# Two half-filled score units become one: the last 64 queries of two neighbouring head pairs share a unit

## The chip, the cores and the metric

The kernel runs on one core of one Trainium2 chip. The metric is the device time of one execution in microseconds (us). Three timed executions of the kernel before took 1442.98, 1452.02 and 1453.08 us, a median of 1452.02 us. A core has a matrix engine (TensorE, PE in the profile, with its weight loads shown apart as PEld), a vector engine (VectorE, DVE), an activation engine (ScalarE, ACT), GpSimd (POOL), and SyncE (SP), whose queue issues nearly all DMAs here. The engines run their own instruction streams and wait for each other through semaphores.

## The reference

Two stages follow each other. The first is attention with a threshold, for 8 batches of 8 heads, 576 rows of 64 numbers each:

```python
scores = scale * np.matmul(q, k.transpose(0, 1, 3, 2))
thresh = np.max(scores, axis=-1, keepdims=True) - tau
scores = np.where(scores >= thresh, scores, -1000000000.0)
attn = np.exp(scores - np.max(scores, axis=-1, keepdims=True))
attn = attn / (np.sum(attn, axis=-1, keepdims=True) + 1e-09)
return np.matmul(attn, v)
```

Its output, with the heads put side by side, is a matrix x of 4608 rows by 512. The second stage is a bilinear layer with weights w_a and w_b (512 by 1536) and w_out (1536 by 512): `((x @ w_a) * (x @ w_b)) @ w_out`. All of it is in fp32. In the records of this kernel each fp32 matmul appears as two weight loads and two matmuls, so counts in the profile are twice those in the code.

## The kernel before, in words

**Units.** The 64 heads are handled as 32 pairs, with `HP = 4` pairs to a batch. One head of a pair lies on partitions 0 to 63 (j = 0), the other on 64 to 127 (j = 1). The 576 queries of a pair are cut into four units of 128 queries and one tail unit (`u == NT`) of the last 64. The list `units` orders them, 160 in all, and the main loop `for g in range(len(units) + PV_LAG)` gives one slot to each. In the first batch the order is units 0 and 1 of all four pairs, then units 2 and 3 of each, then the four tails. In each later batch it is units 0 and 1 of the four pairs, then units 2, 3 and the tail of each.

**A unit on its engines.** `scores` (L374) issues the score matmuls on PE into PSUM, and the row maxima (L393) and thresholds (L394) on DVE. The array works as four tiles of 64 by 64: the row half is given by the head's partitions, the column half by the partitions written. A full unit has eight matmuls of 288 columns (two halves of the keys c, two groups of 64 queries t, two heads j), one to each tile and half of the keys, and fills two pairs of PSUM banks. A tail unit has only four: head 0 writes partitions 64 to 127 and head 1 writes 0 to 63, so two of the four tiles have no score matmul, and it fills one pair of banks. `weigh` then takes the exponential on ACT (L414) and applies the threshold and sums on DVE (L417); `reciprocal` and `normalise` (L436) follow. From the ninth unit on, the weights are turned by 32x32 transposes on DVE (L480), a DMA to a scratch tensor in DRAM (`turn_blocks`, swap<-tw) and a DMA back (`turn_back`, wT<-swap). Three slots after the scores (`PV_LAG`), `weighted` multiplies by v (`product`, L520) and `settle` copies the result into x tiles. What is weighted in which slot is told by `part`: half 0 of a pair after unit 1, half 1 after unit 3 in the first batch and, together with the tail, after the tail unit in later ones.

**The layer beside it.** The bilinear layer is worked off in 18 blocks of 256 rows of x (`ffn`, `sevens_of`: lines L680, L753, L810, L856). A block becomes available when its x tile is complete: two from each batch, and one more from the tails of four batches. Inside every slot `advance` issues a share of the current block's matmuls between the attention's. The share is `pace`, in moving columns: `PACE` times the columns of a block, held down so that the backlog lasts until the next block arrives (`arrivals`), plus a term for the product's columns and one for a large backlog. In the first slots the weights of the layer are also converted on ACT, POOL and DVE (`early`), some pieces per slot, through slot 15.

**Order and queues.** `keep_order` fixes every engine's instructions in the order in which the Python program issues them. DMAs are collected by `post` and released by `pump` as PE's columns go by, after slot 40; before that they are issued at once. `flush` issues what a step needs immediately. Queries of later batches arrive in two parts, q0 and q1, with `Q_BUFS = 2` buffers, three slots before they are used.

Of the kernel before, what the change touches and what calls it, by code (L numbers as in the profile page):

```python
# [10 lines left out]
FP32 = mybir.dt.float32  # L11
# [12 lines left out]
BY_PE = 8  # L24
XT_BUFS = 7
Q_BUFS = 2
OSB_BUFS = 4
PACE = 0.09
CATCH_UP = 0.05
PACE_EARLY = 0.04  # L30
ROOM = 1024
# [23 lines left out]
def kernel(  # L55
# [288 lines left out]

    prepared, scored, weights, turned, whole = {}, {}, {}, {}, {}
    x_of, xtail_of = {}, {}
    ahead, settled = {}, {}
    blocks, complete, swaps = [], [], {}

    def prep(i, name):  # L350
# [23 lines left out]
    def scores(i, u):  # L374
        qT, kT = prepared[i]["q" if i < HP else "q1" if u > 1 else "q0"], prepared[i]["k"]
        base = HALF if i >= HP and u > 1 else 0
        n = 2 if u < NT else 1
        sc = [banks(SH, "sc") for _ in range(n)]
        each = [(c, t, j) for c in range(2) for t in range(n) for j in range(2)]
        if units.index((i, u)) < BY_HEAD:  # L380
            each.sort(key=lambda x: x[2])
        for c, t, j in each:
            r = slice(j * D, (j + 1) * D)
            o = t if u < NT else 1 - j
            q0, to = (u * P + t * D if u < NT else MAIN) - base, slice(o * D, (o + 1) * D)
            nc.tensor.matmul(sc[j if u < NT else 0][to, c], qT[r, q0:q0 + D],  # L386
                             kT[r, c * SH:(c + 1) * SH], start=True, stop=True)
        mx = small.tile([P, 2], FP32, tag="mx", name="mx")
        thr = small.tile([P, 2], FP32, tag="thr", name="thr")
        bias = small.tile([P, 2], FP32, tag="bias", name="bias")  # L390
        for j in range(n):
            c = slice(j, j + 1)
            nc.vector.tensor_reduce(mx[:, c], sc[j], axis=AX.XY, op=ALU.max)  # L393
        nc.vector.tensor_scalar(thr[:, 0:n], mx[:, 0:n], cut, None, op0=ALU.subtract)  # L394
        scored[i, u] = (sc, thr, bias, mx)

    def rooms_of(i, u):


        t = work.tile([P, 2 * NB, Q], FP32, tag="tw", bufs=TW_BUFS, name="tw")  # L400
        whole[i, u] = t
        return [t[:, j * NB:(j + 1) * NB] for j in range(1 if u == NT else 2)]

    def weigh(i, u):

# [57 lines left out]
            nc.scalar.copy(wT[:, y * NT:(y + 1) * NT], tp[:, y])  # L463
        nc.vector.tensor_copy(wT[:, 2 * NT], last[:, 0])

    def part(i, u):

        if i < HP:
            return {1: (i, 0), 3: (i, 1), NT: (i, 2)}.get(u)
        return {1: (i, 0), NT: (i, 1)}.get(u)  # L470

    def width(i, h):
        return (HALF, HALF, TAIL)[h] if i < HP else (HALF, HALF + TAIL)[h]
# [1 line left out]
    def turn_blocks(i, u):  # L475

        ws, _ = weights.pop((i, u))
        t = whole.pop((i, u))
        for w in ws:
            nc.vector.transpose(w, w)  # L480
        if u < NT:
            swap = scratch.tile([G, P, NSLOT * Q], FP32, tag="swap", name="swap")
        else:
            swap = scratch.tile([2, P, NSLOT * Q], FP32, tag="swapt", name="swap")
        swaps[i, u] = swap
        for g in range(G):
            if u < NT:
                to, n = swap[g], G
            else:
                to, n = swap[g % 2, (1 - g // 2) * D:(2 - g // 2) * D], 2  # L490
            post(("tw", i, u), (to.rearrange("(r p) e -> p r e", p=Q),
                                t[g * Q:(g + 1) * Q, 0:n * NSLOT].rearrange("p (r s) e -> p r (s e)", r=n)))

    def turn_back(i, u):

        flush(("tw", i, u))
        swap = swaps.pop((i, u)).rearrange("g p e -> p g e")
        key = "wT", i, min(u // 2, 1) if i >= HP else u // 2
        if u < NT or i < HP:
            turned[i, u] = turned_tile()  # L500
            n = G if u < NT else 2
            for y in range(0, n, 2):
                post(key, (turned[i, u][:, y:y + 2].rearrange("p g s e -> p g (s e)"), swap[:, y:y + 2]))
        else:
            for y in range(2):
                post(key, (turned[i, 2 + y][:, G].rearrange("p s e -> p (s e)"), swap[:, y]))

    def join(out, lo, hi):
        nc.scalar.copy(out, lo)
# [58 lines left out]
    def weighted_unit(i, u):  # L568

        b, hp = pairs[i]  # L570
        wT = turned.pop((i, u, "pe"))
        pv = product([lambda rows, s, t=t: t[rows, s] for t in wT], loaded[i]["v"], P)
        if (b, 0) not in x_of:
            x_of[b, 0] = x_tile("xT")
            state["xs"] = x_tile("xS")
        settle(x_of[b, 0][:, hp, u * P:(u + 1) * P], pv, 0, D, ([], []))
        exchange(x_of[b, 0], state["xs"], hp, u * P, (u + 1) * P, nc.gpsimd)
        if hp == HP - 1:
            state["rows"] = u + 1
            if u == 0:  # L580
                blocks.append(((x_of[b, 0], state["xs"]), ("first", b, 0)))

    def weighted(i, h):

        b, hp = pairs[i]
        flush(("v", i), ("wT", i, h))
        n = width(i, h)
        if h < 2:
            groups = G + (n > HALF)
            wT = [turned.pop((i, 2 * h + y))[:, 0:groups] for y in range(2)]  # L590
        else:
            t = turned.pop((i, NT))
            wT = [t[:, y:y + 1] for y in range(2)]
        pv = product([lambda rows, s, t=t: t[rows, :, s] for t in wT], loaded[i]["v"], n)
        read = [], []
        if h < 2:
            if hp == 0:
                x_of[b, h] = x_tile("xT")
            settle(x_of[b, h][:, hp, :], pv, 0, P, read)
            settled[b, h] = hp + 1  # L600
            if hp == HP - 1:
                del settled[b, h]
                complete.append((x_of.pop((b, h)), ("half", b, h)))
        if n % HALF:
            t = b % GT
            if hp == 0 and t == 0:
                xtail_of[b // GT] = x_tile("xt")
            settle(xtail_of[b // GT][:, hp, t * TAIL:(t + 1) * TAIL], pv, (n - TAIL) // 2, n // 2, read)
            del loaded[i], prepared[i]
            if hp == HP - 1 and t == GT - 1:  # L610
                complete.append((xtail_of.pop(b // GT), ("tail", b - t, 0)))

# [331 lines left out]
    for i in range(0, NPR, HP):  # L944
        if i == 0:
            units += [(p, u) for u in (0, 1) for p in range(HP)]
            units += [(p, u) for p in range(HP) for u in (2, 3)]
            units += [(p, NT) for p in range(HP)]
        else:
            units += [(p, u) for p in range(i, i + HP) for u in (0, 1)]  # L950
            units += [(p, u) for p in range(i, i + HP) for u in (2, 3, NT)]
    arrivals = [g + PV_LAG + 1 for g, (i, u) in enumerate(units)
                if i % HP == HP - 1 and part(i, u) and (i >= HP or u == NT - 1)]
    first = {i: g for g, (i, u) in enumerate(units) if u == 0}
    second = {i: g for g, (i, u) in enumerate(units) if u == 2}

# [23 lines left out]
        n += size  # L980
    for g in range(len(units) + PV_LAG):
        written = len(pending)
        state["slot"], state["paced"] = g, g > 40
        while bulk and bulk[0][1] < g - 1:
            pump()
        state["converted"] = state["added"]
# [2 lines left out]
        back = ()  # L989
        if BY_PE + 1 < g <= len(units) + 1:  # L990
            n = g - PV_LAG
            back = (1 if BY_PE <= n and part(*units[n]) else 0,)
            if not back[0]:
                turn_back(*units[g - 2])
        if here:
# [4 lines left out]
        pace = (PACE if g > BY_PE else PACE_EARLY) * BLOCK_COLS  # L1000
        if g > BY_PE:
            pace = min(pace, backlog() / (min([a for a in arrivals if a > g] + [len(units) + PV_LAG + 1]) - g))
        pace += NSLOT * S / 2 / (NT + 1) + CATCH_UP * max(backlog() - BLOCK_COLS, 0)
        if 2 <= g < BY_PE + 2:
            weighted_unit(*units[g - 2])
            running["owed"] -= NSLOT * P // 2
# [13 lines left out]
            advance(PORTIONS[0] * pace)  # L1020
        for p in range(HP, NPR):
            for name, d in (("q0", 1), ("q1", 1)):
                if g == (second if name == "q1" else first)[p] - d:
                    prep(p, name)
        if here:
            weigh(i, u)
# [10 lines left out]
        if g > BY_PE:  # L1037
            n = g - PV_LAG
            held = 0.0
            if BY_PE <= n < len(units) and part(*units[n]):  # L1040
                held = 384 - (PORTIONS[2] + PORTIONS[3]) * pace + NSLOT * width(*part(*units[n])) // 2
                held = min(max(held, 0.0), 384)
            advance(PORTIONS[1] * pace - held)
            if BY_PE <= n < len(units) and part(*units[n]):
                p, h = part(*units[n])
                if pairs[p][1] == 0:
                    make_x(2 if h == 1 and p >= HP and pairs[p][0] % GT == 0 else 1)
                make_room()
                weighted(*part(*units[n]))
                passed(NSLOT * width(*part(*units[n])) // 2)  # L1050
                running["owed"] -= NSLOT * width(*part(*units[n])) // 2
            if back and back[0] > 0:
                turn_back(*units[g - 2])
        for n in early.get(g, [])[:1]:
# [14 lines left out]
        load_weights(RAWS)  # L1069
        for p in range(HP, NPR):  # L1070
            for name, d in (("q0", 3), ("k", 4), ("q1", 3)):
                if g == (second if name == "q1" else first)[p] - d:
                    load(p, name)
        for p in range(1, NPR):
            if g == first[p] - 1:
# [63 lines left out]
```

## Time and profile before

| | before |
|---|---|
| timed executions | 1442.98, 1452.02, 1453.08 us |
| profiled execution, first to last instruction | 1439.3 us |
| PE busy | 1386.8 us (96%) |
| PE weight loads busy | 1282.4 us (89%) |
| DVE busy | 1015.6 us (71%) |
| ACT busy | 683.9 us (48%) |
| POOL busy | 480.4 us (33%) |
| score matmul records L386 | 2304, 229.1 us |
| mean granted PE clock | 0.992 |

The total of the profiled execution beyond its span is not listed apart; the shortest timed execution is 3.7 us longer than the span, the median 12.7 us. Busy times of PE are modelled, since matmuls are pipelined: a matmul record of 288 columns is shown with about 405 ns, but up to four run side by side, one per tile. So a group's cost on PE has to be read from the distance between starts, not from its mean duration.

### The profile page before, as it was taken

The page shows a single profiled execution, that of the slowest core. Times are in us where ns is not written, and L with a number is a line of the kernel's source. Part 1 is how long each engine was busy: PE and PEld are TensorE (multiplying, and loading weights), DVE is VectorE, ACT ScalarE, POOL GpSimd, SP SyncE. Part 2 cuts the span into 40 slices and gives each one's busy share as a digit, 9 for nine tenths or more (in the row PEclk, how much of TensorE's full clock was granted, in tenths as well). Part 3 has the DMA queues.
Part 4 walks back from the last instruction along what each step waited for, and adds up shares of the span by engine and source line. Part 5 has one row for each costly group of instructions (what it writes and reads, how often), then busy time and mean ns, then how long its engine had stood idle before and what let it go on. Part 6 is the DMA issues. An engine that isn't in the chain of part 4 may idle for free.

```text
span 1439.3 us, 77100 instructions
## 1 busy us (share of the span) xinstructions
PE 1386.8 (96%) x34208; PEld 1282.4 (89%) x34208; DVE 1015.6 (71%) x2244; ACT 683.9 (48%) x1244; POOL 480.4 (33%) x668
## 2 busy tenths in 40 slices
PE   6888999999999999999999999999999999999998
PEld 5777798988879889989999999898898989999998
DVE  6997778788767877676757786778867776755223
ACT  5876455545545454544444545344535454430110
POOL 2763713415060605132333333240506060605000
PEclk9899999999999999999999999999999999999999
DMA  9975667667755776567545677466755686450000
GB/s 210 252 227 141 173 173 191 182 171 192 202 137 153 176 201 159 152 160 189 147 125 137 159 186 203 118 171 149 207 135 142 164 217 167 121 160 18 3 18 17
DMA packets 327004, 223.25 MB, mean 155 GB/s; under 512 B 171536, under 2 KB 310800, under 8 KB 326672
## 3 DMA queue, kind: packets, MB, share of 16 engines
q1 hardware_dynamic: 324160, 217.74, 58.5%
q8 instruction: 269, 4.41, 1.3%
q10 hardware_dynamic: 2512, 0.59, 0.2%
q14 instruction: 63, 0.52, 0.1%
HBM read 128.58 MB, written 89.65 MB: 152 GB/s over the span
## 4 chain that ended last, share of the span: by engine, by line
PE 88%; DVE 4%; DMA 4%; issue 2%; SPq 2%; ACT 1%; DVEq 0%; ACTq 0%
PE pab L680 27%; PE po L810 20%; PE pab L753 19%; PE sc L386 10%; PE pv L520 10%; PE po L856 1%; DMA wT<-swap 1%; PE tp L461 1%; DVE mx L393 1%; DVE tw L480 1%; SPq L197 1%; DMA raw<-in_moe_w_a_dram 1%; SPq L143 1%; DMA raw<-in_moe_w_b_dram 0%; DVE tw L417 0%
## 5 line engine op out<-in xcount | busy, mean ns | idle before, releaser
L436 ACT ACTIVATE tw<-tw,rcp 128x576 f32<-128x576 f32 x272 | 197.8, 769 | 228.7 <-DVE rcp L430 228.6
L393 DVE TENSOR_REDUCE mx<-sc 128x1 f32<-128x576 f32 x288 | 206.1, 752 | 140.7 <-PE sc L386 115.6
L414 ACT ACTIVATE tw<-sc,bias,scalars 128x576 f32<-128x576 f32 x288 | 239.4, 831 | 9.8 <-ACT bias L413 0.2
L646 POOL TENSOR_TENSOR h<-h,u 128x512 f32<-128x512 f32 x28 | 35.1, 1276 | 604.2 <-DVE h L723 465.4
L810 PE MATMUL po<-wo_sb,h 64*64 64x256 f32 x3264 | 230.8, 377 | 0.0
L417 DVE SCALAR_TENSOR_TENSOR tw<-sc,thr,tw 128x576 f32<-128x576 f32 x288 | 222.6, 797 | 9.7 <-ACT tw L414 9.1
L386 PE MATMUL sc<-kT,qT 64*64 64x288 f32 x2016 | 198.1, 405 | 7.2 <-issue 2.9
L480 DVE STREAM_TRANSPOSE tw<-tw 128x576 f32<-128x576 f32 x272 | 196.0, 754 | 0.8 <-ACT tw L436 0.8
L810 PEld LDWEIGHTS po<-wo_sb,h 64*64 64x64 f32 x3264 | 178.7, 133 | 15.8 <-DVE h L723 0.3
L520 PE MATMUL pv<-wT,vm 64*64 64x160 f32 (+3 forms) x5184 | 181.7, 273 | 7.1 <-issue 4.3
L520 PEld LDWEIGHTS pv<-wT,vm 64*64 64x64 f32 x5184 | 167.7, 134 | 13.9 <-issue 6.8
L810 PE MATMUL po<-sums_u,h 64*64 64x256 f32 x2448 | 169.6, 377 | 0.3 <-DVE h L761 0.3
L779 POOL TENSOR_TENSOR h<-h 128x256 f32<-128x256 f32 x168 | 117.4, 733 | 119.8 <-PE po L810 116.1
L386 PEld LDWEIGHTS sc<-kT,qT 64*64 64x64 f32 x2016 | 119.5, 133 | 31.9 <-issue 10.6
L810 PEld LDWEIGHTS po<-sums_u,h 64*64 64x64 f32 x2448 | 132.2, 133 | 12.5 <-DVE h L761 1.2
L680 PE MATMUL pab<-xU,wb_sb 64*64 64x128 f32 x4096 | 138.5, 270 | 0.1
L680 PEld LDWEIGHTS pab<-xU,wb_sb 64*64 64x64 f32 x4096 | 131.0, 133 | 2.2 <-issue 0.5
L413 ACT ACTIVATE bias<-mx,scalars 128x1 f32<-128x1 f32 x288 | 83.3, 289 | 92.5 <-DVE mx L393 92.3
L680 PE MATMUL pab<-xS,wa_sb 64*64 64x128 f32 x2048 | 113.1, 270 | 1.2 <-issue 1.2
L753 PE MATMUL pab<-xS,wb_sb 64*64 64x256 f32 (+1 forms) x1536 | 102.9, 359 | 4.1 <-issue 4.1
L527 ACT COPY xT<-pv 128x128 f32<-128x128 f32 (+1 forms) x68 | 17.6, 259 | 187.2 <-PE pv L520 152.6
L753 PE MATMUL pab<-xS,wa_sb 64*64 64x256 f32 (+1 forms) x1536 | 101.4, 361 | 0.0
(138 smaller groups left out, 2427.7 us busy)
## 6 DMA issues: line engine op xcount, KB each, us to landing
wT<-swap SPq DMA_DIRECT2D x244, 288.0 KB, 3.8
swap<-tw SPq DMA_DIRECT2D x480, 144.0 KB, 2.9
vm<-in_v_dram SPq DMA_DIRECT2D x128, 72.0 KB, 2.8
swap<-tw SPq DMA_DIRECT2D x128, 72.0 KB, 3.1
kT<-in_k_dram SPq DMA_DIRECT2D x112, 72.0 KB, 3.1
wT<-swap SPq DMA_DIRECT2D x56, 144.0 KB, 2.6
out_dram<-kept SPq DMA_DIRECT2D x30, 256.0 KB, 3.5
qT<-in_q_dram SPq DMA_DIRECT2D x112, 40.0 KB, 2.6
```

The source lines that it names most:

```text
L386: nc.tensor.matmul(sc[j if u < NT else 0][to, c], qT[r, q0:q0 + D], kT[r, c * SH:(c + 1) * SH], start=True, stop=True)
L393: nc.vector.tensor_reduce(mx[:, c], sc[j], axis=AX.XY, op=ALU.max)
L413: nc.scalar.activation(bias[:, j:j + 1], mx[:, j:j + 1], AF.Copy, scale=e_nscale)
L414: nc.scalar.activation(wb[j], sb[j], AF.Exp, bias=bias[:, j:j + 1], scale=e_scale)
L417: nc.vector.scalar_tensor_tensor(out=wv, in0=sb[j], scalar=thr[:, j:j + 1], in1=wv, op0=ALU.is_ge, op1=ALU.mult, accum_out=sums[:, j:j + 1])
L436: nc.scalar.activation(w, w, AF.Copy, scale=rcp[:, j:j + 1])
L480: nc.vector.transpose(w, w)
L520: nc.tensor.matmul(pv[c * D:(c + 1) * D, y], vm[rows, s], wT[y](rows, s), start=(s == 0), stop=(s == NSLOT - 1))
L680: nc.tensor.matmul(out[c * D:(c + 1) * D, r, f * P:(f + 1) * P], w[g][k][rows, w0:w0 + D], moving[k][rows], start=(fresh and k == 0 and f ...
L753: nc.tensor.matmul(pab[c * D:(c + 1) * D, r], w[rows, f // n, k, fs + c * D:fs + (c + 1) * D], moving, start=(k == 0), stop=(k == H - 1))
L779: (nc.vector if state["over"] else nc.gpsimd).tensor_tensor(*a, **kw)
L810: nc.tensor.matmul(po[c * D:(c + 1) * D, r, y], ht[rows, t0:t0 + D], other[rows, f], start=(f == 0), stop=(f == NF // 2 - 1))
```

## The change

The tail units of pairs p and p + 1 (p even) become one unit. It has eight matmuls of 288 columns: pair p + t writes the PSUM banks `sc[t]`, and head j of it the partitions `(j ^ t) * 64` on, so that all four tiles have score matmuls. All steps after that handle two banks as in a full unit. The joint unit stands in the list after unit 3 of the even pair: 2, 3, tail, then 2, 3 of the odd pair, in the first batch too, where the four tails stood at the end. There are 144 units instead of 160. In later batches the odd pair's half 1 and tail are now weighted after its unit 3, and its tail's scratch is read back in that unit's `turn_back`; in the first batch both pairs' tails are weighted three slots after the joint unit. The second part of an odd pair's queries is loaded and transposed one slot earlier. `PACE` becomes 0.1, the term for the product's columns follows the number of units, and the paced DMAs begin after slot 36.

```diff
-PACE = 0.09
+PACE = 0.1
 def scores(i, u):
-        n = 2 if u < NT else 1
-        sc = [banks(SH, "sc") for _ in range(n)]
-        each = [(c, t, j) for c in range(2) for t in range(n) for j in range(2)]
+        sc = [banks(SH, "sc") for _ in range(2)]
+        each = [(c, t, j) for c in range(2) for t in range(2) for j in range(2)]
...
-            o = t if u < NT else 1 - j
-            q0, to = (u * P + t * D if u < NT else MAIN) - base, slice(o * D, (o + 1) * D)
-            nc.tensor.matmul(sc[j if u < NT else 0][to, c], qT[r, q0:q0 + D],
+            if u < NT:
+                m, o, q0 = j, t, u * P + t * D - base
+            else:
+                m, o, q0 = t, j ^ t, MAIN - base
+                qT, kT = prepared[i + t]["q" if i < HP else "q1"], prepared[i + t]["k"]
+            nc.tensor.matmul(sc[m][o * D:(o + 1) * D, c], qT[r, q0:q0 + D],
                              kT[r, c * SH:(c + 1) * SH], start=True, stop=True)
...
-    def part(i, u):
+    def parts(i, u):
         if i < HP:
-            return {1: (i, 0), 3: (i, 1), NT: (i, 2)}.get(u)
-        return {1: (i, 0), NT: (i, 1)}.get(u)
+            return {1: [(i, 0)], 3: [(i, 1)], NT: [(i, 2), (i + 1, 2)]}.get(u, [])
+        return {1: [(i, 0)], NT if i % 2 == 0 else 3: [(i, 1)]}.get(u, [])
...
 def turn_back(i, u):
+        if i >= HP and u == (3 if i % 2 else NT):
+            flush(("tw", i - i % 2, NT))
+            swap = swaps[i - i % 2, NT].rearrange("g p e -> p g e")
             for y in range(2):
-                post(key, (turned[i, 2 + y][:, G].rearrange("p s e -> p (s e)"), swap[:, y]))
+                post(key, (turned[i, 2 + y][:, G].rearrange("p s e -> p (s e)"), swap[:, i % 2 * 2 + y]))
...
         if i == 0:
             units += [(p, u) for u in (0, 1) for p in range(HP)]
-            units += [(p, u) for p in range(HP) for u in (2, 3)]
-            units += [(p, NT) for p in range(HP)]
+            units += [(p, u) for p in range(HP) for u in ((2, 3) if p % 2 else (2, 3, NT))]
         else:
             units += [(p, u) for p in range(i, i + HP) for u in (0, 1)]
-            units += [(p, u) for p in range(i, i + HP) for u in (2, 3, NT)]
+            units += [(p, u) for p in range(i, i + HP) for u in ((2, 3) if p % 2 else (2, 3, NT))]
...
-        state["slot"], state["paced"] = g, g > 40
+        state["slot"], state["paced"] = g, g > 36
...
-        pace += NSLOT * S / 2 / (NT + 1) + CATCH_UP * max(backlog() - BLOCK_COLS, 0)
+        pace += NSLOT * S / (2 * NT + 1) + CATCH_UP * max(backlog() - BLOCK_COLS, 0)
...
-                if g == (second if name == "q1" else first)[p] - d:
+                if g == (second if name == "q1" else first)[p] - d - (name == "q1" and p % 2):
```

More of the change, by code (lines that the diff above doesn't have):

```diff
@@ L346 @@
     x_of, xtail_of = {}, {}
-    ahead, settled = {}, {}
+    ahead, settled, settled_of = {}, {}, {}
     blocks, complete, swaps = [], [], {}
@@ L390, in scores @@
         bias = small.tile([P, 2], FP32, tag="bias", name="bias")
-        for j in range(n):
+        for j in range(2):
             c = slice(j, j + 1)
             nc.vector.tensor_reduce(mx[:, c], sc[j], axis=AX.XY, op=ALU.max)
-        nc.vector.tensor_scalar(thr[:, 0:n], mx[:, 0:n], cut, None, op0=ALU.subtract)
+        nc.vector.tensor_scalar(thr, mx, cut, None, op0=ALU.subtract)
         scored[i, u] = (sc, thr, bias, mx)
@@ L401, in rooms_of @@
         whole[i, u] = t
-        return [t[:, j * NB:(j + 1) * NB] for j in range(1 if u == NT else 2)]
+        return [t[:, j * NB:(j + 1) * NB] for j in range(2)]
     def weigh(i, u):
@@ L480, in turn_blocks @@
             nc.vector.transpose(w, w)
[L481 to L484, printed above, removed]
+        swap = scratch.tile([G, P, NSLOT * Q], FP32, tag="swap" if u < NT else "swapt", name="swap")
         swaps[i, u] = swap
@@ L487, in turn_blocks @@
             if u < NT:
-                to, n = swap[g], G
-            else:
-                to, n = swap[g % 2, (1 - g // 2) * D:(2 - g // 2) * D], 2
-            post(("tw", i, u), (to.rearrange("(r p) e -> p r e", p=Q),
-                                t[g * Q:(g + 1) * Q, 0:n * NSLOT].rearrange("p (r s) e -> p r (s e)", r=n)))
+                moves = [(swap[g].rearrange("(r p) e -> p r e", p=Q),
+                          t[g * Q:(g + 1) * Q].rearrange("p (r s) e -> p r (s e)", r=G))]
+            else:
+                moves = []
+                for m in range(2):
+                    j = g // 2 ^ m
+                    moves.append((swap[2 * m + g % 2, j * D:(j + 1) * D].rearrange("(r p) e -> p r e", p=Q),
+                                  t[g * Q:(g + 1) * Q, m * NB:(m + 1) * NB].rearrange("p (r s) e -> p r (s e)", r=2)))
+            post(("tw", i, u), *moves)
     def turn_back(i, u):
-        flush(("tw", i, u))
-        swap = swaps.pop((i, u)).rearrange("g p e -> p g e")
         key = "wT", i, min(u // 2, 1) if i >= HP else u // 2
         if u < NT or i < HP:
+            flush(("tw", i, u))
+            swap = swaps.pop((i, u)).rearrange("g p e -> p g e")
             turned[i, u] = turned_tile()
-            n = G if u < NT else 2
-            for y in range(0, n, 2):
+            for y in range(0, G, 2):
                 post(key, (turned[i, u][:, y:y + 2].rearrange("p g s e -> p g (s e)"), swap[:, y:y + 2]))
-        else:
+        if i >= HP and u == (3 if i % 2 else NT):
+            flush(("tw", i - i % 2, NT))
+            swap = swaps[i - i % 2, NT].rearrange("g p e -> p g e")
             for y in range(2):
-                post(key, (turned[i, 2 + y][:, G].rearrange("p s e -> p (s e)"), swap[:, y]))
+                post(key, (turned[i, 2 + y][:, G].rearrange("p s e -> p (s e)"), swap[:, i % 2 * 2 + y]))
+            if i % 2:
+                del swaps[i - 1, NT]
     def join(out, lo, hi):
@@ L572, in weighted_unit @@
         pv = product([lambda rows, s, t=t: t[rows, s] for t in wT], loaded[i]["v"], P)
+        settled_of[i] = settled_of.get(i, 0) + P
         if (b, 0) not in x_of:
@@ L585, in weighted @@
         b, hp = pairs[i]
-        flush(("v", i), ("wT", i, h))
+        flush(("v", i), ("wT", i if i >= HP or h < 2 else i - i % 2, h))
         n = width(i, h)
@@ L591, in weighted @@
         else:
-            t = turned.pop((i, NT))
-            wT = [t[:, y:y + 1] for y in range(2)]
+            t = turned[i - i % 2, NT]
+            wT = [t[:, i % 2 * 2 + y:i % 2 * 2 + y + 1] for y in range(2)]
+            if i % 2:
+                del turned[i - 1, NT]
         pv = product([lambda rows, s, t=t: t[rows, :, s] for t in wT], loaded[i]["v"], n)
         read = [], []
+        settled_of[i] = settled_of.get(i, 0) + n
+        if settled_of[i] == S:
+            del loaded[i], prepared[i]
         if h < 2:
@@ L608, in weighted @@
             settle(xtail_of[b // GT][:, hp, t * TAIL:(t + 1) * TAIL], pv, (n - TAIL) // 2, n // 2, read)
-            del loaded[i], prepared[i]
             if hp == HP - 1 and t == GT - 1:
@@ L946 @@
             units += [(p, u) for u in (0, 1) for p in range(HP)]
-            units += [(p, u) for p in range(HP) for u in (2, 3)]
-            units += [(p, NT) for p in range(HP)]
+            units += [(p, u) for p in range(HP) for u in ((2, 3) if p % 2 else (2, 3, NT))]
         else:
             units += [(p, u) for p in range(i, i + HP) for u in (0, 1)]
-            units += [(p, u) for p in range(i, i + HP) for u in (2, 3, NT)]
+            units += [(p, u) for p in range(i, i + HP) for u in ((2, 3) if p % 2 else (2, 3, NT))]
     arrivals = [g + PV_LAG + 1 for g, (i, u) in enumerate(units)
-                if i % HP == HP - 1 and part(i, u) and (i >= HP or u == NT - 1)]
+                if i % HP == HP - 1 and parts(i, u) and (i >= HP or u == NT - 1)]
     first = {i: g for g, (i, u) in enumerate(units) if u == 0}
@@ L991 @@
             n = g - PV_LAG
-            back = (1 if BY_PE <= n and part(*units[n]) else 0,)
+            back = (1 if BY_PE <= n and parts(*units[n]) else 0,)
             if not back[0]:
@@ L1039 @@
             held = 0.0
-            if BY_PE <= n < len(units) and part(*units[n]):
-                held = 384 - (PORTIONS[2] + PORTIONS[3]) * pace + NSLOT * width(*part(*units[n])) // 2
+            now = parts(*units[n]) if BY_PE <= n < len(units) else []
+            if now:
+                held = 384 - (PORTIONS[2] + PORTIONS[3]) * pace + NSLOT * sum(width(*x) for x in now) // 2
                 held = min(max(held, 0.0), 384)
             advance(PORTIONS[1] * pace - held)
-            if BY_PE <= n < len(units) and part(*units[n]):
-                p, h = part(*units[n])
+            for p, h in now:
                 if pairs[p][1] == 0:
@@ L1048 @@
                 make_room()
-                weighted(*part(*units[n]))
-                passed(NSLOT * width(*part(*units[n])) // 2)
-                running["owed"] -= NSLOT * width(*part(*units[n])) // 2
+                weighted(p, h)
+                passed(NSLOT * width(p, h) // 2)
+                running["owed"] -= NSLOT * width(p, h) // 2
             if back and back[0] > 0:
@@ L1071 @@
             for name, d in (("q0", 3), ("k", 4), ("q1", 3)):
-                if g == (second if name == "q1" else first)[p] - d:
+                if g == (second if name == "q1" else first)[p] - d - (name == "q1" and p % 2):
                     load(p, name)
```

## The prediction

> **What bounds the kernel now.** I read the page's busy row first, then the waits of PE, then the stages, and at last the timeline around single units.
>
> ```profile
> PE 1386.8 (96%) x34208; PEld 1282.4 (89%) x34208; DVE 1015.6 (71%) x2244; ACT 683.9 (48%) x1244; POOL 480.4 (33%) x668
> PE 88%; DVE 4%; DMA 4%; issue 2%; SPq 2%; ACT 1%; DVEq 0%; ACTq 0%
> ```
>
> PE is busy for 96% of the span, and the chain of work that ended last lies on PE for 88% of it. So whatever shortens PE's stream should shorten the kernel, and whatever only helps another engine should not. The stages show where the other 4% are (columns: stretch, its length, then busy time of PE, PEld, DVE, ACT and POOL with their instructions, PE's granted clock, the DMA engines' share, GB/s):
>
> ```profile
> 84.00:148.00 64.00, 53.57 (x1317) 46.15 (x1309) 53.27 (x109) 43.73 (x87) 32.46 (x34) 0.97 0.69 189
> 148.00:176.00 28.00, 28.00 (x457) 22.39 (x450) 19.02 (x45) 11.60 (x22) 21.21 (x19) 1.00 0.65 159
> 176.00:346.00 170.00, 165.46 (x3870) 152.50 (x3863) 138.44 (x315) 90.62 (x166) 62.56 (x78) 1.00 0.69 180
> 346.00:1276.00 930.00, 919.53 (x23239) 851.56 (x23233) 679.47 (x1512) 457.75 (x814) 297.77 (x447) 1.00 0.63 164
> 1276.00:1440.00 164.00, 157.50 (x4038) 156.50 (x4032) 59.58 (x110) 19.25 (x35) 21.67 (x34) 0.99 0.10 28
> ```
>
> I cut them at the starts of units, taken from the score matmuls in the timeline: the tenth unit starts at 84, the first of the four tails at 148, the first unit of the second batch at 176, the last unit at 1276. After 346 PE idles about 1%. The idle time is in the first 148 us, where the layer's weights are converted and units take some 9 us each.
>
> **Part 1: the score matmuls.** The change issues the same number of instructions on PE. Two tails have 2 x 4 matmuls, the joint unit has 8; only their placing on tiles differs. So I need the price of a tail and that of a full unit in PE time. The first three lines below that name L386 are one tail; L680 is the layer's work around it:
>
> ```profile
> 441.42 0.44 PE L386 MATMUL sc<-kT,qT 64*64 64x288 f32 x2
> 441.47 0.43 PE L680 MATMUL pab<-xU,wb_sb 64*64 64x128 f32 x2
> 441.66 0.68 PE L386 MATMUL sc<-kT,qT 64*64 64x288 f32 x4
> 441.95 0.44 PE L680 MATMUL pab<-xU,wb_sb 64*64 64x128 f32 x4
> 442.15 0.44 PE L386 MATMUL sc<-kT,qT 64*64 64x288 f32 x2
> 442.39 0.81 PE L680 MATMUL pab<-xU,wb_sb 64*64 64x128 f32 x19
> ...
> 535.60 1.15 PE L386 MATMUL sc<-kT,qT 64*64 64x288 f32 x16
> 536.57 1.05 PE L680 MATMUL pab<-xU,first_u 64*64 64x128 f32 x32
> ```
>
> The tail's 8 records start two at a time and hold their two tiles from 441.42 to 442.39, 0.97 us. A full unit's 16 records hold four tiles from 535.60 to 536.57, also 0.97 us. If the other two tiles stood idle, each pair of tails would shrink from 1.94 to 0.97 us: 16 x 0.97 = 15.5 us saved. But six records of L680 start between the tail's. A row of the chain gives their rate, 754.74 to 761.82 for 244 of them, 29.0 ns each, so 0.17 us of the 0.97 is used, and this tail costs 0.80 us. I did the same sum for every unit that has only layer matmuls on both sides (time between the middles of the two neighbouring runs, less their records at 27.7 ns for 128 columns and 55.4 for 256): 28 tails cost 0.75 us in the median and in the mean, 55 full units 0.93 in the median and 1.09 in the mean, the latter with their waits. A pair of tails against one joint unit saves 2 x 0.75 - 0.93 = 0.57 or, by means, 1.50 - 1.09 = 0.41 us; times 16, 9.1 or 6.6 us. **I take 8 us.** The ends are 15.5 (nothing runs beside a tail) and -2 (a tail costs only half of 0.97 because its neighbours fill the array, and a joint unit costs 1.09 with the waits of a full one: 0.97 - 1.09 = -0.12, times 16).
>
> The Trainium skill, "TensorE: Matmul & The Clock Gate", Part 3 (Packing small matmuls), says that matmuls keep program order in start and end. Taken strictly, nothing could run beside a tail's second half, and the saving would be the 15.5 us; the row above, with L680 records starting at 441.95 before score records at 442.15, speaks against it. "TensorEngine Tiling (Array Packing)", Gotcha 1, says that different row tiles cannot access one PSUM bank simultaneously. The joint unit has head 0 and head 1 of a pair write two halves of one bank, where a full unit gives each head its own, so by this rule it would run at half rate and cost 1.94 us.
>
> The tail now already writes both heads into one bank, and its records start in twos. The product (L520) places its four tiles in the same diagonal way; 72 of its records with 160 columns cost 2.49 us there, about 34.6 ns each, the same per column as 55.4 for 256. So I put no price on the shared bank.
>
> **Part 2: DVE and ACT.** Large instructions stay the same in number (288 maxima at 752 ns, 288 of L417 at 797, 272 transposes at 754). Forty-eight small ones go, 16 each of the threshold (302 ns), the sum's addend (231) and the reciprocal (165): 11 us of DVE in total. DVE is 71% busy and idle beside PE after 176 us, so I count 0; at most the reciprocals ahead of L436 give 16 x 0.17 = 3 us.
>
> **Part 3: what moves.** In the later batches the odd pair loses the spare slot between its last turned tile and its product. Four DMAs (two of 288 KB, two of 144 KB) land in the slot ahead of the product instead of two plus two. Landing takes 3.8 us in the median against slots of 7 to 9 us, and half 0 of every pair is treated in this way already: PE waits for wT<-swap once, 0.4 us in all. So 0; without that cover it is up to 3.8 us for each of 14 odd pairs. On SP's queue the number of DMAs is the same; a joint unit posts eight at once. Their order is by PE's columns, and its packets take 58.5% of the DMA engines. The query part q1 of the odd pair comes a slot earlier, and its buffer was released by the scores of that same slot, as now.
>
> The first batch matters more. Now it has 20 slots before the second batch starts; then it has 18. The second block of the layer arrives with slot 19 now, and with slot 21 then, because half 1 of the last pair comes after both joint units. `pace` spreads the first block over more slots. In the instruction orders as built, the layer's matmuls ahead of the second batch fall from 39,168 to 29,184 moving columns. At 54.0 ns per 256-column record (128 records of L810 in 6.91 us) and 8 records per 256 columns, 9,984 columns are 16.8 us of PE, put off until later. Attention work up to there is the same but for Part 1. The question is by how much this stretch gets shorter. It is 92 us now (84 to 176) with 81.6 us of PE and 72.3 of DVE. Units 10 to 16 keep their conversion, so I leave them 64 us; two more full units follow at 7 to 8 us, DVE about 6: 79 us. It ends 13 us earlier with 17 us less done: **+4 us**. With DVE packed without gaps (72 us) it is -3, with 9.1 us for all nine units (82) +7, with nothing gained (92) +17.
>
> Later slots are more even: no light tail slots, some 8 to 9.5 us of PE work each instead of 4 to 8. Short slots are those in which PE waits for a PSUM pair to be released. In 176 to 346 PE idles 4.5 us; I take **-2** of it, from 0 to -4.
>
> **Sum.** -8 + 0 + 4 - 2 = -6 us; with every end on one side it is -15.5 - 3 - 3 - 4 = -26 or 2 + 17 = +19 us. The profiled execution spans 1439.3 us, so 1433 is expected for its span. The median of the timed runs is 12.7 us above that span and their spread is 10 us, so the same difference against the median gives **1446 us**. About 1%, 14.5 us, is what a measurement of this kernel can tell from no change.
>
> **The rivals.**
> - *No neighbour really fills the tails, and the start costs nothing* (faster by over 1%). For it: the tail's two tiles are held 0.97 us as long as a full unit's four, and what runs beside may only be a few matmuls taken ahead, given back at the next wait. -15.5 - 3 - 2 = -20 us, 1432. Against: median 0.75 over 28 tails.
> - *The layer's work thins out ahead of the second block* (slower). It decides from the point at which the second batch's first unit starts later than about 167 us (176 less 17 of work put off, plus the 8 of Part 1). If that start stays at 176, PE loses 17 us and regains 8: +9 us, 1461; beyond 182 it is over 1%. For it: PE is already idle for 10.4 of 64 us there, with DVE 83% busy. Against: the conversion ends by slot 15, and 148 to 176 runs PE at 28.00 of 28.
> - *The shared bank makes row tiles take turns.* A joint unit then costs 1.94 us against 1.50 for two tails: +7 us, and the change doesn't do what it says; with +4 and -2 1461. Against: the product's rate.
>
> **Chances.** Forecast (-14 to +3) 0.53; first rival 0.27; thinning 0.15, a third of it over 1%; shared bank 0.05. Half of what is left of each lies inside 1%, so faster by over 1% is 0.30, within 1% 0.59, slower by over 1% 0.11. The range 1430 to 1461 takes in the rivals' centres and leaves the ends beyond.
>
> **What would show it.** In the changed profile: joint units with 16 records in about 1 us and no layer records inside them; the second batch's first score near 163 us (right), or 176 (thinning); PE busy lower by about 8 us with an idle share no larger; no wait of L520's counterpart on wT<-swap. The prediction is wrong if joint units last near 2 us, if the stretch to the second batch keeps its length, or if slots of equal weight cost PE more waits on PSUM than now.

## The result, and the profile after

The changed kernel took 1427.16 us in the median of four timed executions (1424.32 to 1429.98), the kernel before 1449.26 us in the same comparison (1442.98 to 1453.08). The ratio is 0.9856, with a 95% interval of 0.9815 to 0.9898. In a second comparison, with 5 executions of the changed kernel and 15 of the one before on one chip, it was 1424.57 against 1444.22 us, a ratio of 0.9873 (0.9852 to 0.9894). So, by the ratios, the change saves 18 to 21 us, 1.3 to 1.4%. The forecast was 6 us and 1446 us, with a range from 1430: the direction was right, the size was three times too small, and the time lies just below the range.

The profiled execution spans 1425.2 us and took 1427.02. That is 14.1 us less than the span before. The profile of before had a good start: its first nine units took 76.0 us (first scores at 8.1, those of the tenth unit at 84.1), where the same instructions took 77 to 82 us in every other profile of this study. Comparisons of times below therefore go by ratios of timed executions, and the profiles tell where the time went. With this start left out, from the tenth unit to the end, the profile before took 1355.2 us and the two of the changed kernel 1337.0 and 1337.3, 18 us less.

The page of the changed kernel, the busy row and the shares of the chain that ended last:

```profile
PE 1369.9 (96%) x34208; PEld 1237.2 (87%) x34208; DVE 1007.7 (71%) x2196; ACT 679.4 (48%) x1244; POOL 480.7 (34%) x668
PE 83%; DVE 6%; DMA 5%; SPq 3%; issue 2%; ACT 1%; DVEq 0%; ACTq 0%
```

PE has the same 34,208 records, is busy 16.9 us less, and is still 96% of the span: the kernel is bound as before, by a stream that takes PE less time. DVE lost exactly 48 instructions and 8 us (11 us in the second profile). The stages, with the same columns as before, are cut again at the starts of units: the tenth at 88, the first of the second batch at 159, the last joint unit at 1237.

```profile
88.00:159.00 71.00, 62.87 (x1588) 53.79 (x1581) 66.22 (x142) 52.22 (x102) 41.15 (x43) 0.98 0.78 200
159.00:346.00 187.00, 182.15 (x4045) 165.13 (x4041) 144.64 (x321) 94.69 (x173) 74.66 (x89) 0.99 0.71 181
346.00:1237.00 891.00, 880.28 (x22511) 785.12 (x22507) 653.85 (x1436) 439.42 (x791) 289.66 (x436) 1.00 0.64 166
1237.00:1425.00 188.00, 182.12 (x4760) 179.98 (x4752) 73.38 (x143) 31.64 (x57) 28.35 (x44) 0.99 0.16 45
```

PE idles 10.7 of 891 us in the long third stage, 1.2%, as much as before (10.5 of 930). The stretch from the tenth unit to the second batch takes 71 us instead of 92. A joint unit in the timeline of PE:

```profile
240.48 1.79 PE L821 MATMUL po<-wo_sb,h 64*64 64x256 f32 x28
241.99 1.25 PE L388 MATMUL sc<-kT,qT 64*64 64x288 f32 x16
242.96 1.14 PE L821 MATMUL po<-wo_sb,h 64*64 64x256 f32 x16
```

Its 16 records hold the array from 241.99 to 242.96, 0.97 us, with no layer matmul among them. That is what a full unit takes, and what each of two tails took before. Eleven of the 16 joint units look like this one; among the scores of the other five start one to five layer records.

### The profile page after: what moved, and what is told of

Its sections match the earlier page's. It is cut to its first block, busy times and chain, and to the rows that moved or that the text cites. A ratio compares the mean times of both kernels' runs of the same rounds, so it can differ in the third digit from the quotient of the medians.

```text
span 1425.2 us, 76956 instructions
## 1 busy us (share of the span) xinstructions
PE 1369.9 (96%) x34208; PEld 1237.2 (87%) x34208; DVE 1007.7 (71%) x2196; ACT 679.4 (48%) x1244; POOL 480.7 (34%) x668
## 4 chain that ended last, share of the span: by engine, by line
PE 83%; DVE 6%; DMA 5%; SPq 3%; issue 2%; ACT 1%; DVEq 0%; ACTq 0%
PE pab L691 27%; PE po L821 21%; PE pab L764 17%; PE pv L526 10%; PE sc L388 9%; SPq L143 2%; DVE mx L395 1%; DVE tw L482 1%; DMA vm<-in_v_dram 1%; DMA wT<-swap 1%; DVE tw L419 1%; DMA qT<-in_q_dram 1%; DMA sums_u<-in_moe_w_b_dram 1%; DMA raw<-in_moe_w_a_dram 1%; SPq L266 0%
## 5 line engine op out<-in xcount | busy, mean ns | idle before, releaser
L821 PE MATMUL po<-wo_sb,h 64*64 64x256 f32 x3264 | 208.3, 376 | 1.2 <-DVE h L734 1.1
L821 PEld LDWEIGHTS po<-wo_sb,h 64*64 64x64 f32 x3264 | 157.7, 133 | 26.5 <-DVE h L734 2.6
L526 PEld LDWEIGHTS pv<-wT,vm 64*64 64x64 f32 x5184 | 160.7, 135 | 19.5 <-issue 11.1
L526 PE MATMUL pv<-wT,vm 64*64 64x160 f32 (+3 forms) x5184 | 170.8, 274 | 6.8 <-DMA wT<-swap 3.3
L388 PE MATMUL sc<-kT,qT 64*64 64x288 f32 x2016 | 168.5, 405 | 2.2 <-DVE xt L534 1.6
L821 PE MATMUL po<-sums_u,h 64*64 64x256 f32 x2448 | 155.1, 376 | 0.7 <-DVE h L772 0.7
L821 PEld LDWEIGHTS po<-sums_u,h 64*64 64x64 f32 x2448 | 117.2, 133 | 21.3 <-DVE h L772 1.7
L388 PEld LDWEIGHTS sc<-kT,qT 64*64 64x64 f32 x2016 | 102.2, 134 | 22.8 <-issue 4.9
L534 DVE COPY xT<-pv 64x128 f32<-64x128 f32 (+1 forms) x136 | 38.2, 281 | 92.3 <-PE pv L526 90.8
L691 PE MATMUL pab<-xS,wa_sb 64*64 64x128 f32 x2048 | 96.5, 269 | 0.4 <-issue 0.4
```

The costliest lines, as they stand in the source:

```text
L388: nc.tensor.matmul(sc[m][o * D:(o + 1) * D, c], qT[r, q0:q0 + D], kT[r, c * SH:(c + 1) * SH], start=True, stop=True)
L526: nc.tensor.matmul(pv[c * D:(c + 1) * D, y], vm[rows, s], wT[y](rows, s), start=(s == 0), stop=(s == NSLOT - 1))
L691: nc.tensor.matmul(out[c * D:(c + 1) * D, r, f * P:(f + 1) * P], w[g][k][rows, w0:w0 + D], moving[k][rows], start=(fresh and k == 0 and f ...
L821: nc.tensor.matmul(po[c * D:(c + 1) * D, r, y], ht[rows, t0:t0 + D], other[rows, f], start=(f == 0), stop=(f == NF // 2 - 1))
```

## The experiments

### The joint unit on two tiles

The joint unit stays, but its matmuls go to the two tiles that tails used.

```diff
-                m, o, q0 = t, j ^ t, MAIN - base
+                m, o, q0 = t, 1 - j, MAIN - base
...
-                    j = g // 2 ^ m
+                    j = 1 - g // 2
```

> The changed kernel, but the joint unit's eight score matmuls all go to the two tiles that a tail used before (both pairs put head j on the partitions of 1 - j; the scratch copies follow). Order, units, pace and all other instructions stay. Theory A (the four tiles give some 8 us, the rest of the 14 to 22 us comes from fewer, evener units): a joint unit costs about 2 x 0.75 us as two tails do, 16 x (1.50 - 0.93) = 9 us back, so 8 to 12 us over the changed kernel (1435 to 1440) and still 6 to 12 us under the kernel before. Rival B (the four tiles give all of it, nothing ran beside a tail): 16 to 20 us back, within 0.3% of the kernel before. Rival C (tiles give nothing): within 3 us of the changed kernel.

Measured: 1437.84 us (1432.45 to 1441.36), ratio 0.9961 (0.9939 to 0.9984). Against 0.9873 for the changed kernel that is 0.0088 of 1445 us, 12.7 us, with some 4 us of uncertainty. Theory A's 9 us is somewhat small, B's 16 to 20 too much, and C is out. A joint unit of this kernel:

```profile
246.66 1.39 PE L388 MATMUL sc<-kT,qT 64*64 64x288 f32 x10
247.66 0.43 PE L821 MATMUL po<-wo_sb,h 64*64 64x256 f32 x1
247.88 0.42 PE L388 MATMUL sc<-kT,qT 64*64 64x288 f32 x2
247.92 0.38 PE L821 MATMUL po<-wo_sb,h 64*64 64x256 f32 x1
248.12 0.42 PE L388 MATMUL sc<-kT,qT 64*64 64x288 f32 x2
248.14 0.43 PE L821 MATMUL po<-wo_sb,h 64*64 64x256 f32 x2
248.36 0.42 PE L388 MATMUL sc<-kT,qT 64*64 64x288 f32 x2
248.41 0.65 PE L821 MATMUL po<-wo_sb,h 64*64 64x256 f32 x5
```

For its first microsecond, from 246.66 to 247.66, only score matmuls start, although two tiles are free. Layer matmuls come in only beside the last six records. All 14 joint units of the later batches look like this: the first layer record starts 0.98 to 1.02 us after the first score (once 1.29), beside the last six. So the free tiles are filled near the end of a group, not along it.

### A tail's and a joint unit's matmuls twice

In the kernel before, and in the changed kernel, the score matmuls of a tail or a joint unit are issued a second time and write the same products again.

```diff
-        for c, t, j in each:
+        for c, t, j in each * (2 if u == NT else 1):
```

> The kernel before with each tail's four score matmuls issued twice (the same products written again), nothing else. It prices the two-tile form by itself: 32 more sets. If nothing runs beside them: 32 x 0.97 = 31 us slower. If the neighbours fill half of the free tiles (the 0.75 us of the prediction): 24 us. If they fill all: 16 us.

> The changed kernel with each joint unit's eight score matmuls issued twice. It prices the four-tile form by itself: 16 more sets of 0.88 to 0.97 us, 14 to 16 us slower than the changed kernel. If heads that write one bank took turns, 1.94 us each: 31 us.

Measured: with tails twice 1475.64 us against 1444.22, ratio 1.0231 (1.0203 to 1.0259): 31.4 us for 32 sets, 0.98 us each, with some 0.13 of uncertainty. With joint units twice 1440.08 us, ratio 0.9974 (0.9954 to 0.9994), against 1424.57: 15.5 us for 16 sets, 0.97 us each, with some 0.26. A set of eight records on two tiles costs as much as one of sixteen on four: nothing runs beside it, unless it is the end of its group. The traces say the same: in 26 of the 28 doubled tails of later batches the first layer record starts 0.98 to 1.11 us after the first score, again beside the last six records. And the two heads that write one bank do not take turns: that would have cost 31 us, not 15.5.

### The old pace, the paced DMAs, and the new pace in the kernel before

The changed kernel with both old constants, with the old start of the paced DMAs alone, and the kernel before with both new ones.

```diff
-PACE = 0.1
+PACE = 0.09
...
-        state["slot"], state["paced"] = g, g > 36
+        state["slot"], state["paced"] = g, g > 40
```

> The changed kernel with the old pace (0.09) and the paced DMAs from slot 40 again. Theory A (units and tiles carry the gain; pace only moves the layer's work towards the end, where PE is full too): within 3 us of the changed kernel. Rival D (the new pace is what makes slots evener and saves waits): 5 to 10 us slower than the changed kernel.

> The changed kernel with the paced DMAs from slot 40 again and the new pace kept, so that the two constants are told apart. Theory H: within 2 us of the changed kernel (ratio near 0.987). If the loss with both old constants came from the DMAs, 5 us or more slower.

> The kernel before with the new pace (0.1) and the paced DMAs from slot 36. Its 160 slots stay, so each slot carries a tenth more of the layer's work and less is left for the end (by the instruction order some 19 us less after the last unit). Theory A: within 3 us of the kernel before. Rival D (pace is a source of the gain): 5 us or more faster.

Measured: both old constants 1442.67 us, ratio 0.9991 (0.9969 to 1.0013). The old DMA start alone 1427.90 us, ratio 0.9875 (0.9830 to 0.9919). The kernel before with both new ones 1435.29 us, ratio 0.9950 (0.9924 to 0.9977). So theory A falls and Rival D's direction stands, with more than its 5 to 10 us. The two constants together are worth 0.0118 of 1445 us, 17 us, in the changed kernel; without them hardly anything of the change is left. The DMA start by itself shows no difference (0.9875 against 0.9873, with some 7 us of uncertainty), so the 17 us are called the pace's from here on, though no run put back the pace alone. In the kernel before the new constants give 7 us. The pace is a share per slot: 0.09 over 160 slots and 0.1 over 144 both come to 14.4 blocks. The starts of the units tell where the 17 us lie. With the old constants 10,736 more moving columns of the layer, 18 us at eight records to 256 columns and 54.0 ns each, start behind the last unit's first score, and from there to the end it takes 189.4 us instead of 171.6. The slots from the second batch to that unit carry that much less, yet they shrink only from 1094.3 to 1089.9 us, and PE's idle time in them grows from 15.7 to 23.7 us. In the kernel before, the same move of work by the new constants costs the slots about what it saves behind them: 163.2 to 145.1 us at the end, 1099.6 to 1117.0 us in the slots (one profile of each kernel, which do not show all of the 7 us that the timed executions do).

The waits of PE's weight loads from 176 us on (waiting engine and line, what ended the wait, total us, times, longest), first of the changed kernel, then with the old constants:

```profile
PEld sc L388 <- issue: 4.2, 7, 1.8
...
PEld pv L526 <- issue: 2.5, 8, 0.9
```

```profile
PEld pv L526 <- issue: 13.2, 13, 1.8
PEld sc L388 <- issue: 6.8, 13, 1.2
```

The products' waits grow from 2.5 to 13.2 us. "Issue" says that the profile shows no releaser. I took the time from the start of the last layer matmul ahead of each product to the product's first: for products of 160 columns, those with half 1 and the tail, it sums to 14.9 us with the old constants and 4.4 with the new. One of them in the timeline of all engines:

```profile
309.46 1.93 PE L764 MATMUL pab<-xT,wa_sb 64*64 64x256 f32 x30
...
310.68 1.25 DVE L730 TENSOR_TENSOR u<-u,pab 128x512 f32<-128x512 f32 x2
311.85 0.80 DVE L419 SCALAR_TENSOR_TENSOR tw<-sc,thr,tw 128x576 f32<-128x576 f32 x1
...
312.76 0.72 PE L526 MATMUL pv<-wT,vm 64*64 64x160 f32 x11 [1.37 <-issue]
```

The layer's matmuls run out at 311.4. DVE reads the first PSUM pair of the same slot's scores until 312.65, and the product starts at 312.76. There are four PSUM pairs, of which a full or joint unit's scores hold two until DVE has read them. Ten of the 28 products start over 0.3 us after the last layer matmul. Six of these, 9.7 of the 14.9 us, start 0.11 us after the end of DVE's read of the first PSUM pair of the slot's scores; the other four, 3.0 us, start 0.05 us after DVE has read a PSUM pair of the layer. No wT<-swap transfer lands in the last microsecond before any of the ten, so it isn't the turned weights that they wait for. In the kernel before, the 160-column products of later batches stood in the next pair's tail slot for three pairs of four, with scores that hold one PSUM pair.

### More or less of the layer ahead of the product

The shares of a slot's layer work were changed, in the changed kernel with the old constants, in the changed kernel, and in the kernel before.

```diff
-PORTIONS = (0.3, 0.35, 0.15, 0.2)
+PORTIONS = (0.3, 0.5, 0.1, 0.1)
```

> The changed kernel with the old pace (0.09, paced DMAs from slot 40) and more of each slot's layer work ahead of the product: the shares of a slot become 0.3, 0.5, 0.1, 0.1 in place of 0.3, 0.35, 0.15, 0.2. With the old pace the products of 160 columns waited 14.9 us in all (10 of 28 over 0.3 us), and the one looked at ended when DVE had read the first PSUM pair of the same slot's scores (L419). Theory H (the product then starts before its PSUM pair is free, and the new pace pays by putting more work ahead of it): the wait goes without the new pace, 8 us or more faster than with the old pace alone (1432 or less). Rival I (the new pace pays by how much work it leaves for the end): as slow as with the old pace alone, within 3 us of the kernel before.

> The changed kernel with the same shares 0.3, 0.5, 0.1, 0.1. Its products of 160 columns wait 4.4 us in all and those of 128 columns 3 to 4 us. Theory H: 0 to 4 us faster than the changed kernel (ratio 0.984 to 0.987); if the work taken from behind the product leaves the next slot's scores waiting instead, slower by 2 us or more.

> The kernel before with the shares 0.3, 0.5, 0.1, 0.1. Its products of 160 columns stand in tail slots, where only one PSUM pair is held by scores, and wait 2.8 us in all; those of 128 columns 5.5 us. Theory H: little to gain, 0 to 5 us faster. If it gains 10 us or more, the waits on PSUM are more than the profile shows.

Measured: 1457.05 us, ratio 1.0077 (1.0049 to 1.0105), with the old constants; 1437.74 us, ratio 0.9940 (0.9920 to 0.9960), in the changed kernel; 1452.71 us, ratio 1.0045 (1.0017 to 1.0073), in the kernel before. All three lose, by 12, 10 and 6 us. Theory H falls in the form in which I put it, and so does rival I, which had the first of them unchanged. The local part of H came out: with the old constants the 160-column products waited 3.4 us instead of 14.9. But the waits moved. The same view from 176 us on, old constants and late shares:

```profile
PEld sc L388 <- issue: 16.4, 28, 1.9
PEld pv L526 <- issue: 6.7, 10, 1.8
PEld pab L691 <- issue: 6.3, 14, 0.9
PEld pab L691 <- DVE u L730: 5.4, 6, 1.9
```

The scores now wait 16.4 us where they waited 6.8: layer work taken from behind the product is missing ahead of the next slot's scores. That fits the loss, and it would be why moving the work does not replace a larger pace; the rows do not add up to the whole 12 us. Then the opposite, less ahead of the product, in the changed kernel:

```diff
-PORTIONS = (0.3, 0.35, 0.15, 0.2)
+PORTIONS = (0.3, 0.25, 0.2, 0.25)
```

> The changed kernel with less of each slot's layer work ahead of the product: shares 0.3, 0.25, 0.2, 0.25. With more ahead of it (0.3, 0.5, 0.1, 0.1) the changed kernel lost 13 us, although its products waited less, because scores and layer matmuls waited more. Theory J (a slot's layer work has to cover two chains, one ahead of the product and one behind it; the shares as they are lie between): the products of 160 columns wait again, some 10 us, and the kernel is 5 us or more slower than the changed one. If what lies behind the product is the scarcer part (theory K): 3 us or more faster (ratio 0.985 or less).

Measured: 1432.27 us, ratio 0.9892 (0.9858 to 0.9927). The 160-column products waited 6.0 us, not 10. A loss of 3 us by the ratios, whose intervals overlap: neither theory is settled by it, though K's gain is out.

### A still larger pace

```diff
-PACE = 0.1
+PACE = 0.11
```

> The changed kernel with the pace at 0.11 in place of 0.1, so that about 23 us of the layer's work move from behind the last unit into the slots. If the pace works by filling slots that would otherwise wait (theory D, after the old pace lost 15 us or more of the gain), there is a little more to get or nothing: between 1418 and 1428, 0 to 6 us faster than the changed kernel. If 0.1 is already past the point where slots wait (theory F), the same within 2 us. If the layer's blocks run out in the slots (rival G), slower by 3 us or more.

Measured: 1427.89 us, ratio 0.9897 (0.9870 to 0.9924), 3 us above the changed kernel, with intervals that overlap. Theory D's further gain is not seen. The 3 us lie between theory F (the same within 2 us) and rival G (slower by 3 or more), and the runs don't tell these two apart; either way a pace above 0.1 gains nothing. No version in this study beat the changed kernel.

### Two tiles and the old pace at once

Both edits above together, the two tiles and the old constants.

> Both undone at once: the joint unit on two tiles, and the pace 0.09 with paced DMAs from slot 40. If the tiles' 13 us and the pace's 17 us do not depend on each other, the ratio is 0.9991 + 0.0088 = 1.008, 11 us slower than the kernel before. If the old pace's waits hide a longer joint unit (PE idles there in any case): 1.000 to 1.003.

Measured: 1458.96 us, ratio 1.0082 (1.0052 to 1.0113). The four tiles are worth 0.0088 with the new pace and 0.0091 with the old: they add up. The pace is worth 17 us on four tiles and 0.0121, 17 us, on two. So joining the units, on two tiles and with the old constants, by itself costs 12 us.

### The tails early in the first batch

One part of the change in the kernel before: in the first batch each tail follows its pair's unit 3.

```diff
-            units += [(p, u) for p in range(HP) for u in (2, 3)]
-            units += [(p, NT) for p in range(HP)]
+            units += [(p, u) for p in range(HP) for u in (2, 3, NT)]
```

> The kernel before with one part of the change: in the first batch each pair's tail unit follows its unit 3, as in the later batches, instead of all four at the end. The layer's work ahead of the second batch falls by some 12 us of PE, as in the change (17 us). The recorded prediction's step (work put off there is only partly regained): 3 to 5 us slower than the kernel before. Theory A after the result (the stretch shortens by as much as is put off): within 2 us of it. Rival E (the reorder itself is a source of the gain): 3 us or more faster.

Measured: 1440.82 us, ratio 0.9974 (0.9953 to 0.9995), 3.7 us faster than the kernel before. The step on record (3 to 5 us slower) is refuted, and Rival E fits: the reorder is a small gain. The interval, 0.7 to 7 us, does not exclude theory A (within 2 us). In its profile the second batch starts at 168.0 us where it started at 176.5. The stretch from the tenth unit to there shortens by 10.3 us, for 11.7 us of the layer's work put off (6,912 moving columns at the same 54.0 ns), and the later slots grow by 9.0 us. So this run's gain doesn't show in the stretch itself.

### The changed kernel again

> The changed kernel as it is, measured on the same chip as the others of this set. 16 to 22 us under the kernel before (the first comparison gave a ratio of 0.986).

Measured: the ratio 0.9873 given at the top. In this profile the second batch starts at 156.5 us and the tenth unit at 85.5, the same 71 us apart as in the first profile.

## Why the prediction was wrong

Three terms of the sum failed: the scores (8 us, where 11 to 13 were measured), the first batch (+4, where about -3 came out), and the pace, which the sum left at nothing and which is worth 17 us.

**What bounds the kernel** was right: PE stays at 96% busy, and the gain is the loss of PE time.

**Part 1, the scores, was right in mechanism and too small in size.** The term was 8 us; the four tiles measured 12.7 and 13.1 us (two pairs of kernels). Those compare with one group of sixteen records on two tiles, whose end is filled once. For two tails apart the sum of the prediction can be repeated closer in: 16 to 24 layer records on each side of a unit instead of the middles of whole runs, and each at the median rate of 32 alike in a row, 27.3 ns for 128 columns and 54.0 for 256. A tail then costs 0.83 us in the mean (0.81 to 0.82 in the median) and a joint unit 0.92 to 0.94 (0.91), and sixteen times the difference is 11 to 12 us. The same sum gives 1.74 us for a joint unit on two tiles, 13 us for sixteen, as timed. Both prices of the prediction were off the same way: a tail was taken at 0.75, a joint unit in the mean of 0.93 and 1.09. One reason is the rate: at 27.7 and 55.4 ns, the records of the long runs beside a unit were credited with more time than they take, although the prediction itself used 54.0 elsewhere. The doubled tails show the limit of the credit for neighbours: inside a group nothing runs beside it. The first rival's 15.5 us was too much by the ends of the groups, which do fill.

**The ends and rules around it.** The shared bank costs nothing (0.97 us a set, so that rival is out, and the rule that the prediction quoted for it does not bind these writes), as the product's rate had said. The strict order in start and end that the Trainium skill states ("TensorE: Matmul & The Clock Gate", Part 3, Packing small matmuls) does not hold in these records: at 247.66 us of the two-tile kernel a layer record starts ahead of six score records that the program issues before it. But what the prediction drew from that order, that the free tiles stay idle, is right for all but the last six records of a group.

**Part 2** was right: 48 small DVE instructions went, and no row ties a shorter wait on PE to them.

**Part 3, the odd pair's lost spare slot**, held nearly at 0: PE's waits for wT<-swap came to 3.3 us in two places (0.8 us of it after 176 us), and to 1.8 us in one place in the second profile, against a single 0.4 before, where the up to 3.8 us for each of 14 pairs would have been 53.

**The first batch failed in sign.** The step said that 16.8 us of work is put off for a stretch that gets only 13 us shorter, +4. The stretch from the tenth unit to the second batch got 21 us shorter (92.4 to 71.1, and 71.0 in the second profile), so -4 and, without the two joint units' own 1 to 1.5 us, about -3. The two slots behind the conversion took 11.5 to 11.8 us where I had allowed 15, and the seven before them 59.3 to 59.4 where I had kept 64. The reorder alone gave -3.7 us as timed, but not in this stretch, so that the place of this gain is not settled. The rival that made this step worse (the second batch still at 176) is out.

**A term was missing: the pace.** The diff raised `PACE` with the smaller number of slots, and the sum carried it at nothing, inside "later slots are more even, -2". It is worth 17 us here, with joint units on four tiles or on two, against 7 us in the kernel before. What the runs show of the reason: with the old constants 18 us of the layer's work is left for the end, the slots shrink by 4 us only, and the waits of the 160-column products, most of them for the PSUM pairs of their own slot's scores, go from 4.4 to 14.9 us. That this comes from the light tail slots, which the joined units take away, fits these rows, but no run tested it by itself; nor are all 17 us found in the waits. The prediction named that kind of wait and took it at a gain of 0 to 4 us. With the new pace the waits are about what they were, so that in the sum "-2" stands for nothing that the runs can separate.

**The sum.** -11 to -12 for the scores and -3 for the start are 14 to 15 of the 18 to 21 us. The rest, some 3 to 7 us, is not assigned by a run of its own. The kernel before also gains 7 us from the new constants, so part of it may be the pace itself, beyond keeping the slots filled; that is argued, not shown. The time on record was also set against a median of three executions, 1452.02 us, where larger sets of the same kernel gave 1444 to 1447; of the 19 us by which 1446 is too high, some 6 come from that. The 12.7 us between span and median were no fixed cost: every execution with a span listed takes about 1.8 us more than its span, and the rest was a fast profiled execution against slower timed ones. The range ended at 1430, 2 us below the centre of the first rival, while its own most favourable sum, -26, would have given 1426.

## What to carry to other kernels

Price a half-filled group of matmuls by issuing it twice: here a set on two of four tiles cost 0.98 us and on four 0.97. Then give credit for the group's end, where neighbours do come in beside the last six records: a tail by itself cost 0.83 us, so that pairing saved some 0.7 us and not the whole set. When units are merged, the number of slots falls and a filler that is dosed per slot has to be dosed anew; price that constant as an edit of its own, because here it decided whether 20 us or nothing was gained. And when a wait is removed by moving filler work ahead of it, look at once at the wait behind: the products' waits went from 14.9 to 3.4 us, and the kernel lost 12 us.

## What the hardware showed that was not expected

Layer matmuls start beside a group of score matmuls only near the group's end: in the two-tile joint unit none starts for 1.0 us while two tiles are free, and then layer records come in beside the last six. Two heads writing the two partition halves of one PSUM bank ran at the rate of heads with a bank each, 0.97 us for sixteen records of 288 columns. And identical first instructions took 76 to 82 us for the first nine units from one execution to the next, a difference of up to a third of the effect that was to be measured.
